# Order of the low parts, of the routing lists and of the blocks in a sliding-window attention and mixture-of-experts kernel

## The chip, the cores and the metric

The kernel runs on one core of one Trainium2 chip. The metric is the device time of one execution in microseconds; a run's time is compared by medians. One execution was also profiled.

## The reference

Attention over 8 batches, 8 heads, 576 positions and 64 dimensions with a window of 64 positions, then a mixture of 8 experts over the 4608 rows that come out, each row going to its two best experts:

```python
scores = scale * np.matmul(q, k.transpose(0, 1, 3, 2))
mask = (rel >= 0) & (rel < window)
attn = softmax(np.where(mask, scores, -1e9));  x = rows of attn @ v      # N=4608, DM=512
noisy_logits = x @ w_gate + np.log1p(np.exp(x @ w_noise)) * noise
top2, top2_w = the two largest of 8 and their softmax
for e in range(E):
    h = np.maximum(x[mask] @ w1[e], 0.0)                                 # 512 -> 1024
    out[mask] += top2_w[mask, k, None] * (h @ w2[e])                     # 1024 -> 512
```

## The kernel before

Attention and routing take the first 193 us and are not touched. What follows is 8 layers, one an expert, the experts 1 to 7 in the order of their load. A layer e has three chunks c of 384, 384 + tail and 384 rows (the tail has 64 rows in layers 0 to 2, 32 in layers 3 and 4, none in layers 5 to 7). A chunk (e,c) is an *up* (`up`, L799) and a *down* (`down`, L863).

Every product is made of three matmuls: high by high, high by low, low by high. A high part is ScalarE's copy of a value into fp32r (`split`, L214), the low part is VectorE's subtraction of the high one from the value (L215). So each value that goes into a matmul has an ACT instruction and, behind it, a DVE instruction that waits for it.

The up has 8 pieces `o` of 4 steps of 3 matmuls (L820 to L822), each piece into one of three `ps_u` banks. After a piece ACT writes `hh` (L826), DVE `hl` (L830, L832), and for the tail `ht` (L834, L835). In layers 1 to 7 the chunks 1 and 2 are *paired*: two row tiles are multiplied in seven blocks instead of eight halves. For these, `raw` (L841, L844 to L847) and its parts `sh`, `sl` (L848 by way of `split`) are made in the up, and `th`, `tl` from sums of the weights (`mix_w2`, L224).

The down is, unpaired, one `whole` (L876) for each row tile of 128 rows. Paired, it is first the tail's `whole`, then the blocks `p2` and `p`, then four steps of the third tile, the blocks of `s0`, `p5`, `s1` and `s3`, the rest of the third tile, and the last block. The three `ps_d` banks are handed out in the order in which `acc_bank` is called, and so are the three `yo` row tiles. The tail's result is read by ACT (L895) and then by DVE (L896); a block's result is scaled by ACT (`scaled`, L927) or scaled and added by DVE (`added_to`, L930). `add_rows` (L853) adds a row tile into the output by an indirect DMA on POOL.

A chunk's rows are gathered by indirect DMAs on POOL (`gather`, L733), five of them in the down two chunks earlier and the rest in the up of the chunk before, and turned in the down before the chunk's own up (`turn`, L751): a transpose `xy` by DVE (L760), `xh` by ACT (L772), `xl` by DVE (L775).

The list of rows of the expert of rank r is made by `top_list` (L621): 23 small DVE instructions, 9 marks (one-hot tiles, L664), 36 small matmuls over the marks (`put`, L658), then `no`, `hi`, `lo` (L676 to L678; the profile calls `hi` and `lo` `thi` and `tlo`), eight tiny matmuls (`four`, L684, L685) and the index tile `ixs` (L691). It is a generator in `pending`, advanced by `drain` (L978): each call takes n instructions from it; a number that it yields makes it pass over so many calls; `due` holds matmuls with the call at which they are issued. After attention a number is first looked up in `LATE`.

All order is written out by hand: `spread` (L75) sends the steps of an up or a down to PE and, between them, the side work of `parts` at the share of the steps that each part names. Each engine works through its own instructions in the order of the program. The loop over the chunks (L1216) puts the side work together: weight cuts, turns, gathers, mixes, weight loads on SP's queue and the drains.

Of the kernel before, what the change touches and what calls it, by code (L numbers as in the profile page):

```python
# [59 lines left out]
HALF = 8  # L60
# [25 lines left out]
def tile_kernel(ctx, tc, qT, kT, vx, wgx, noise, w1, w2, out):  # L86
# [133 lines left out]

    def split_w2():
        return [lambda f=f: split(stage[:, f % 4, f // 4], W2["h"][:, f], W2["l"][:, f]) for f in ORDER]

    def mix_w2(i):  # L224
        x = stage[:, i].rearrange("p a (b d) -> p a b d", b=2)
        sums = [(x[:, 0, 0], x[:, 0, 1], x[:, 0, 0]), (x[:, 0, 1], x[:, 1, 1], x[:, 0, 1]),
                (x[:, 1, 1], x[:, 1, 1], x[:, 0, 0]), (x[:, 1, 0], x[:, 1, 0], x[:, 1, 1])]
        return ([lambda t=t: nc.vector.tensor_tensor(*t, op=OP.subtract) for t in sums]
                + [lambda a=a: split(stage[:, i, a], W2["th"][:, i, a], W2["tl"][:, i, a]) for a in range(2)])
# [391 lines left out]
    def top_list(e):  # L621
# [38 lines left out]
        for a in range(0, NT, HALF):  # L660
            b = min(NT, a + HALF)
            t = exa.tile([128, 4, 128], F32, name="xy", bufs=2).bitcast(BF).rearrange("p a (b l) -> p (a b) l", l=128)
            for q in range(a, b, 4):
                yield lambda q=q, t=t, a=a: nc.vector.tensor_tensor(  # L664
                    t[:, q - a:q - a + 4], lane[:, None, :].to_broadcast([128, 4, 128]),
                    ln[:, q:q + 4, None].to_broadcast([128, 4, 128]), op=OP.is_equal)
            due.append((calls[0] + LATE["due"], lambda t=t, a=a, b=b: put(t, a, b)))
        yield LATE["due"] + 2
# [12 lines left out]
        def four():  # L681
            for g in range(4):
# [3 lines left out]
        due.append((calls[0] + 2, four))  # L686
# [3 lines left out]
        yield 3  # L690
        yield lambda: nc.vector.tensor_scalar(ALL["ix"][:, e - 1].rearrange("p z g -> p g z"), all4, 4.0, quarter,  # L691
                                              op0=OP.mult, op1=OP.add)

    pending, due, gath = [], [], []
    PACE = {}

# [54 lines left out]
    def turn(e, c):  # L751
# [17 lines left out]

        def g(q, m):  # L770
            h, l = (x[:, :, q * 128:q * 128 + m].rearrange("p k (t c) -> p k t c", c=32) for x in (xh, xl))
            nc.scalar.activation(h, cur[q], AF.Copy)  # L772
            if work.index((e, c)) > 3:
                PACE["t"] = xh.bitcast(F32)[0:1, 0, q * 128:q * 128 + 1]
            nc.vector.tensor_tensor(l, cur[q], h.bitcast(F32), op=OP.subtract)  # L775
        return [lambda q=q, m=m, x=x: x(q, m) for q, m in tiles(e, c) for x in (f, g)]
# [22 lines left out]
    def up(e, c):  # L799
# [6 lines left out]
        raw = {}  # L806
        for o in range(KF):
# [25 lines left out]
            if tail:  # L833
                nc.scalar.activation(t[:, 0], p[:, main:n], AF.Relu)  # L834
                nc.vector.scalar_tensor_tensor(t[:, 1], p[:, main:n], 0.0, t[:, 0].bitcast(F32),  # L835
                                               op0=OP.max, op1=OP.subtract)
            if mix:
                i = f % 4
                if f < 4:
                    x = raw[i] = MIX["p"].tile([128, 4, 128], F32, name="raw", bufs=2)  # L840
                    nc.scalar.activation(x[:, 0:2], p[:, 0:256].rearrange("p (r c) -> p r c", r=2), AF.Relu)  # L841
                else:
                    x = raw.pop(i)
                    nc.vector.scalar_tensor_tensor(x[:, 2], p[:, 128:256], 0.0, x[:, 1], op0=OP.max, op1=OP.add)  # L844
                    nc.vector.tensor_tensor(x[:, 1], x[:, 0], x[:, 1], op=OP.subtract)
                    nc.vector.tensor_tensor(x[:, 0], x[:, 2], x[:, 0], op=OP.subtract)
                    nc.vector.scalar_tensor_tensor(x[:, 3], p[:, 0:128], 0.0, x[:, 0], op0=OP.max, op1=OP.subtract)  # L847
                    split(x, *(y[:, i] for y in SH[e, c]))  # L848
            yield
# [13 lines left out]
    def down(e, c):  # L863
# [12 lines left out]
        def whole(q, m):  # L876
            wt, y, p = weight(q, m), row_tile(), acc_bank()
# [28 lines left out]
        for q, m in tiles(e, c)[3:]:  # L906
            yield from whole(q, m)
# [3 lines left out]
        ws, ys = [weight(q, 128) for q in range(2)], [row_tile() for _ in range(2)]  # L911
# [34 lines left out]
        scaled(lo, p, 0)  # L946
        added_to(lo, p2, 0)
        yield
        for _ in range(4):
            next(third)  # L950
            yield
# [3 lines left out]
        p5 = acc_bank()[:, lo]  # L955
# [22 lines left out]
    def drain(n, bank=True):  # L978
# [3 lines left out]
        while n and pending and calls[0] > calls[1]:  # L982
# [233 lines left out]
    for n, (e, c) in enumerate(work):  # L1216
# [17 lines left out]
        elif n == 1:  # L1234
            pending.extend([start(2), count(), top_list(1), count2()])
            side += [lambda: drain(3), lambda: (drain(3), drain_slots(1, gath))] * 16
        elif c == 0:
            side += split_w2()
        elif c == 1 and e:
            parts0.append((0.0, 0.6, mix_w2(3) + [lambda: load_w1(e + 1, slice(3, 4))]))  # L1240
# [13 lines left out]
        if last and e + 1 < E:  # L1254
            cuts = split_w1()
            for i in range(4):
                side += cuts[2 * i:2 * i + 2] + [lambda i=i: load_w2(e + 1, i)]
# [79 lines left out]
```

## Time and profile before

| | |
|---|---|
| median of 3 runs | 1084.17 us (1082.07 to 1087.49) |
| the profiled execution's own time | 1082.79 us |
| its span, first to last instruction | 1081.1 us |
| PE, matmuls | 1006.5 us busy, 93% |
| PEld, weight loads | 902.6 us, 83% |
| DVE | 707.1 us, 65% |
| ACT | 473.8 us, 44% |
| POOL | 537.0 us, 50% |

The engines are PE (TensorE's matmuls), PEld (its weight loads), DVE (VectorE), ACT (ScalarE), POOL (GpSimd) and SP (SyncE, here only a DMA queue). A tile's name stands before `<-`, what it is made from behind it; L and a number is a line of the kernel before. A matmul's end is modelled, so matmuls overlap in a timeline, and their starts are what counts. An engine that is not the bound may stand idle at no cost.

### The profile page before, as it was taken

The page shows a single profiled execution, that of the slowest core. Times are in us where ns is not written, and L with a number is a line of the kernel's source. Part 1 is how long each engine was busy: PE and PEld are TensorE (multiplying, and loading weights), DVE is VectorE, ACT ScalarE, POOL GpSimd, SP SyncE. Part 2 cuts the span into 40 slices and gives each one's busy share as a digit, 9 for nine tenths or more (in the row PEclk, how much of TensorE's full clock was granted, in tenths as well). Part 3 has the DMA queues.
Part 4 walks back from the last instruction along what each step waited for, and adds up shares of the span by engine and source line. Part 5 has one row for each costly group of instructions (what it writes and reads, how often), then busy time and mean ns, then how long its engine had stood idle before and what let it go on. Part 6 is the DMA issues. An engine that isn't in the chain of part 4 may idle for free.

```text
span 1081.1 us, 23842 instructions
## 1 busy us (share of the span) xinstructions
PE 1006.5 (93%) x9253; PEld 902.6 (83%) x9253; DVE 707.1 (65%) x1716; ACT 473.8 (44%) x1141; POOL 537.0 (50%) x763
## 2 busy tenths in 40 slices
PE   8888889989999899989998999989999999999996
PEld 7777778878898789878987889888898888989895
DVE  6668887773866766666666767576668666467541
ACT  4877784312344344432544245324443453354331
POOL 5432230313865457636663757455666465656411
PEclk9999999989999999999999999999999999999998
DMA  9877897632434134513541344314353335342222
GB/s 318 264 243 230 264 325 272 183 117 38 108 85 108 32 74 106 110 42 47 130 104 48 52 111 86 87 28 106 68 130 50 102 69 115 54 114 48 43 33 30
DMA packets 60667, 123.62 MB, mean 114 GB/s; under 512 B 9728, under 2 KB 9856, under 8 KB 60416
## 3 DMA queue, kind: packets, MB, share of 16 engines
q1 hardware_dynamic: 40816, 83.18, 23.5%
q0 software_dynamic: 19728, 38.82, 21.2%
q8 instruction: 75, 1.23, 0.5%
q14 instruction: 48, 0.39, 0.1%
HBM read 81.59 MB, written 40.37 MB: 113 GB/s over the span
## 4 chain that ended last, share of the span: by engine, by line
PE 56%; DVE 21%; ACT 9%; issue 9%; DMA 3%; POOL 2%; DVEq 0%; ACTq 0%; POOLq 0%
PE ps_d L881 7%; PE ps_d L882 7%; PE ps_d L883 7%; PE ps_u L821 7%; PE ps_u L820 6%; PE ps_u L822 6%; DMA xg<-xrows,ixs 3%; PE ps_d L937 3%; PE ps_d L936 2%; PE ps_d L935 2%; DVE sl L215 2%; DVE hl L832 2%; PE ps_o L334 2%; ACT sh L214 2%; ACT hh L826 2%
## 5 line engine op out<-in xcount | busy, mean ns | idle before, releaser
L746 POOL DMA_INDIRECT xg<-xrows,ixs x258 | 273.4, 1060 | 70.0 <-issue 59.8
L820 PE MATMUL ps_u<-xh,w1h 128*128 128x384 f32 (+2 forms) x752 | 261.6, 348 | 9.8 <-ACT xh L772 5.2
L821 PE MATMUL ps_u<-xl,w1h 128*128 128x384 f32 (+2 forms) x752 | 256.8, 342 | 1.7 <-DVE xl L775 1.7
L822 PE MATMUL ps_u<-xh,w1l 128*128 128x384 f32 (+2 forms) x752 | 256.3, 341 | 0.0
L855 POOL DMA_INDIRECT out_dram<-yo,lts x67 | 118.1, 1763 | 96.4 <-DVE yo L930 54.2
L820 PEld LDWEIGHTS ps_u<-xh,w1h 128*128 128x128 f32 x752 | 141.7, 188 | 17.3 <-ACT xh L772 6.5
L881 PE MATMUL ps_d<-w2h,hh 128*128 128x512 f32 x352 | 141.0, 401 | 12.2 <-DVE yo L896 12.2
L821 PEld LDWEIGHTS ps_u<-xl,w1h 128*128 128x128 f32 x752 | 141.8, 189 | 5.0 <-DVE xl L775 3.2
L832 DVE SCALAR_TENSOR_TENSOR hl<-ps_u,hh 128x384 fp32r<-128x384 f32 x132 | 73.5, 557 | 110.6 <-ACT hh L826 95.6
L826 ACT ACTIVATE hh<-ps_u 128x384 fp32r<-128x384 f32 x188 | 91.4, 486 | 122.4 <-PE ps_u L822 106.6
L822 PEld LDWEIGHTS ps_u<-xh,w1l 128*128 128x128 f32 x752 | 141.6, 188 | 1.5
L882 PE MATMUL ps_d<-w2l,hh 128*128 128x512 f32 x352 | 139.5, 396 | 0.3 <-issue 0.3
L883 PE MATMUL ps_d<-w2h,hl 128*128 128x512 f32 x352 | 139.2, 396 | 0.0
L881 PEld LDWEIGHTS ps_d<-w2h,hh 128*128 128x128 f32 x352 | 67.4, 191 | 25.5 <-DVE yo L896 13.0
L299 POOL TENSOR_TENSOR t<-t,mx 128x512 f32<-128x512 f32 x36 | 37.5, 1042 | 98.9 <-DVE mx L298 74.8
L745 POOL COPY spacer<-hh 1x1 f32<-1x1 f32 x155 | 40.3, 260 | 86.6 <-ACT hh L826 84.9
L883 PEld LDWEIGHTS ps_d<-w2h,hl 128*128 128x128 f32 x352 | 67.2, 191 | 14.4
L214 ACT ACTIVATE sh<-raw 128x512 fp32r<-128x512 f32 x56 | 35.4, 632 | 99.2 <-DVE raw L847 77.3
L882 PEld LDWEIGHTS ps_d<-w2l,hh 128*128 128x128 f32 x352 | 67.3, 191 | 13.2 <-issue 0.7
L772 ACT ACTIVATE xh<-xy 128x512 fp32r<-128x512 f32 (+2 forms) x67 | 41.1, 613 | 71.6 <-DVE xy L760 64.0
L215 DVE TENSOR_TENSOR sl<-raw,sh 128x512 fp32r<-128x512 f32 x56 | 38.8, 692 | 42.4 <-ACT sh L214 37.1
L745 POOL COPY spacer<-xh 1x1 f32<-1x1 f32 x55 | 20.2, 367 | 87.4 <-ACT xh L772 87.2
(273 smaller groups left out, 2056.9 us busy)
## 6 DMA issues: line engine op xcount, KB each, us to landing
stage<-in_w_dram SPq DMA_DIRECT2D x56, 512.0 KB
out_dram<-zero SPq DMA_DIRECT2D x40, 256.0 KB
vw<-in_vx_dram SPq DMA_DIRECT2D x36, 260.0 KB
qc<-in_qT_dram SPq DMA_DIRECT2D x36, 256.0 KB
KW<-in_kT_dram SPq DMA_DIRECT2D x36, 256.0 KB
xrows<-x SPq DMA_DIRECT2D x36, 256.0 KB
xg<-xrows,ixs POOLq DMA_INDIRECT x258
stage<-in_w_dram SPq DMA_DIRECT2D x8, 256.0 KB
```

Source lines behind the costliest of these rows:

```text
L215: eng.tensor_tensor(l, s, h.bitcast(F32), op=OP.subtract)
L745: nc.gpsimd.tensor_copy(spacer, PACE["t"])
L746: nc.gpsimd.indirect_dma_start(out=XG[e, c, t // 4][:, t % 4, :], out_offset=None, in_=XQ[:(DUMP + seen.get((e, c), NT) * 128) * 4], in_of ...
L820: nc.tensor.matmul(p[:, :n], lhsT=w1h[:, k, fs], rhs=xh[:, k, :n], start=(k == 0), stop=False)
L821: nc.tensor.matmul(p[:, :n], lhsT=w1h[:, k, fs], rhs=xl[:, k, :n], start=False, stop=False)
L822: nc.tensor.matmul(p[:, :n], lhsT=w1l[:, k, fs], rhs=xh[:, k, :n], start=False, stop=(k == KD - 1))
L826: nc.scalar.activation(h, p[:, :main], AF.Relu)
L832: nc.vector.scalar_tensor_tensor(l, p[:, :main], 0.0, h.bitcast(F32), op0=OP.max, op1=OP.subtract)
L855: s = nc.gpsimd.indirect_dma_start(out=out[:DUMP + seen.get((e, c), NT) * 128], out_offset=bass.IndirectOffsetOnAxis(ap=slot(e, c, q)[:m, ...
L881: nc.tensor.matmul(p, lhsT=hh[f][:, sl], rhs=w2h[:, f, :], start=(f == 0), stop=False)
L882: nc.tensor.matmul(p, lhsT=hh[f][:, sl], rhs=w2l[:, f, :], start=False, stop=False)
L883: nc.tensor.matmul(p, lhsT=hl[f][:, sl], rhs=w2h[:, f, :], start=False, stop=(f == KF - 1))
```

## The change

- `turn`: in layers 1 to 7 the low part `xl` becomes a step of its own, behind `xh`. Turns are spread over the first 0.75 of the down, not 0.9, and the weight cuts of the next layer beside them over 0.95, where the two followed each other.
- `staged`: weight cuts put out the high part of a piece and then the low part of the piece before. The loads that follow a piece are issued behind its low part.
- `up`: the tail's high part and, for f below 4, `raw` are issued on ACT ahead of DVE's `hl`; the low part of `sh` is owed until the next piece has its `hl`.
- `down`, paired: the third tile's first four steps lead, then the tail, then `p`, `p2` and the rest in the old order. `p2` and `p5` are the two halves of one bank. The row tiles of the two paired tiles are taken after the tail's and the third's.
- `top_list`: marks come in groups of four (`HALF`), one group in three calls, with their matmuls three calls (`PUT`) behind; `four` is due after four calls instead of two. The calls are drawn out from two stretches, down (e,1) and up (e,2), to four: down (e,1) 22 calls, up (e,2) 22, down (e,2) 14, up (e+1,0) 28. The first list is made in chunk (0,1) with two instructions a call.

```diff
-HALF = 8
+HALF = 4
+PUT = 3
+    def staged(cuts, after=lambda k: None):
+        def item(k):
+            if k < len(cuts):
+                nc.scalar.activation(cuts[k][1], cuts[k][0], AF.Copy)
+            if k:
+                nc.vector.tensor_tensor(cuts[k - 1][2], cuts[k - 1][0], cuts[k - 1][1].bitcast(F32), op=OP.subtract)
+                after(k - 1)
+        return [lambda k=k: item(k) for k in range(len(cuts) + 1)]
+    def cut_w1(e):
+        cuts = [tuple(x[:, k, c:c + 512] for x in (w1s, w1h, w1l)) for k in range(KD) for c in range(0, F, 512)]
+        return staged(cuts, lambda k: load_w2(e + 1, k // 2) if k % 2 else None)
...
         for a in range(0, NT, HALF):
...
+            t = exa.tile([128, HALF, 128], BF, name="hot", bufs=2)
+            yield lambda t=t, a=a: nc.vector.tensor_tensor(
+                t, lane[:, None, :].to_broadcast([128, HALF, 128]),
+                ln[:, a:a + HALF, None].to_broadcast([128, HALF, 128]), op=OP.is_equal)
+            due.append((calls[0] + PUT, lambda t=t, a=a: put(t, a, a + HALF)))
+            yield 1
+        yield PUT + 1
...
-        due.append((calls[0] + 2, four))
+        due.append((calls[0] + 4, four))
...
-        yield 3
...
+        yield 6
...
+        steps = (f, g, g2) if e else (f, both)
+        return [lambda q=q, m=m, x=x: x(q, m) for q, m in tiles(e, c) for x in steps]
...
             PACE["t"] = h.bitcast(F32)[0:1, 0:1]
+            if tail:
+                nc.scalar.activation(t[:, 0], p[:, main:n], AF.Relu)
             if mix and f < 4:
+                x = raw[f] = MIX["p"].tile([128, 4, 128], F32, name="raw", bufs=2)
+                nc.scalar.activation(x[:, 0:2], p[:, 0:256].rearrange("p (r c) -> p r c", r=2), AF.Relu)
...
-            if mix:
+            for y in owed:
+                nc.vector.tensor_tensor(*y, op=OP.subtract)
+            owed.clear()
+            if mix and f >= 4:
...
-                    split(x, *(y[:, i] for y in SH[e, c]))
+                nc.scalar.activation(sh, x, AF.Copy)
+                owed.append((sl, x, sh.bitcast(F32)))
...
-        for q, m in tiles(e, c)[3:]:
-            yield from whole(q, m)
+        ends = [whole(q, m) for q, m in tiles(e, c)[3:]]
         third = whole(2, 128)
...
-        ws, ys = [weight(q, 128) for q in range(2)], [row_tile() for _ in range(2)]
+        ws, ys = [weight(q, 128) for q in range(2)], []
...
-        p2 = acc_bank()[:, lo]
-        yield from block(p2, of_h(0, 1), of_w(1, lo))
-        yield
+        for _ in range(4):
+            next(third)
+            yield
+        for x in ends:
+            yield from x
+        ys += [row_tile() for _ in range(2)]
         p = acc_bank()[:, lo]
         yield from block(p, of_h(0, 0), of_w(0, lo))
         scaled(lo, p, 0)
+        yield
+        both = acc_bank()
+        p2, p5 = both[:, lo], both[:, hi]
+        yield from block(p2, of_h(0, 1), of_w(1, lo))
         added_to(lo, p2, 0)
         yield
-        for _ in range(4):
-            next(third)
-            yield
         yield from block(p, of_s(0), of_t(1, hi), False)
         scaled(hi, p, 0)
         yield
-        p5 = acc_bank()[:, lo]
...
-            side += [lambda: drain(3), lambda: (drain(3), drain_slots(1, gath))] * 16
+            side += [lambda: drain(2), lambda: (drain(2), drain_slots(1, gath))] * 16
         elif c == 0:
-            side += split_w2()
+            side += cut_w2()
...
+        if c == 0 and 0 < e < E - 1:
+            parts0.append((0.0, 1.0, [lambda: drain(1)] * 28 + [settle]))
...
-            parts0.append((0.0, 1.0, [lambda: drain(1)] * (30 if e == 0 else 28) + [settle] * (e > 0)))
+            parts0.append((0.0, 1.0, [lambda: drain(1)] * (22 if e else 32)))
...
-        parts = [(0.3, 0.95, side) if nxt and nxt[0] == 0 else (0.0, 0.9, side)]
+        parts = [(0.3, 0.95, side) if nxt and nxt[0] == 0 else (0.0, 0.75, side)] + parts0
...
-            parts.append((0.0, 1.0, [lambda: drain(4)] * 24 + [settle]))
+            parts.append((0.0, 1.0, [lambda: drain(2)] * 32 + [lambda: have(1)]))
...
-            parts.append((0.0, 1.0, [lambda: drain(1)] * 28))
-        if n == 2:
-            parts.append((0.0, 0.9, [lambda: drain(1)] * 24 + [settle]))
+            parts.append((0.0, 1.0, [lambda: drain(1)] * 22))
+        if last and e < E - 2:
+            parts.append((0.0, 1.0, [lambda: drain(1)] * 14))
```

## Rows read from the trace of the kernel before

**Rows 1.** The page: span, busy time and share of each engine.
```profile
span 1081.1 us, 23842 instructions
PE 1006.5 (93%) x9253; PEld 902.6 (83%) x9253; DVE 707.1 (65%) x1716; ACT 473.8 (44%) x1141; POOL 537.0 (50%) x763
```

**Rows 2.** PE's waits: who waited for whom, us in total, times, longest.
```profile
PE ps_d L881 <- DVE yo L896: 12.2, 4, 3.1
PE ps_g L684 <- DVE thi L677: 8.0, 5, 1.6
...
PE ps_u L820 <- ACT xh L772: 5.2, 6, 0.9
PE ps_d L935 <- ACT hh L826: 4.2, 5, 1.3
PE ps_g L658 <- DVE xy L664: 4.1, 4, 2.2
PE ps_d L891 <- DVE ht L835: 3.8, 4, 1.0
PE ps_u L820 <- DVE raw L847: 2.6, 4, 0.9
PE ps_u L821 <- DVE xl L775: 1.7, 6, 0.3
```

**Rows 3.** PE's timeline: start, us, [idle before <- releaser]; up (3,2) and down (7,2).
```profile
619.22 0.34 PE L822 MATMUL ps_u<-xh,w1l 128*128 128x384 f32 x1
621.16 0.17 PE L684 MATMUL ps_g<-thi,same 128*128 128x10 bf16 x1 [1.61 <-DVE thi L677]
...
1056.86 0.28 PE L936 MATMUL ps_d<-w2l,hh 128*128 128x256 f32 x1
1057.23 0.39 PE L937 MATMUL ps_d<-w2h,hl 128*128 128x256 f32 x1
```

**Rows 4.** Windows: stretch, us, busy (x) of PE, PEld, DVE, ACT, POOL; granted clock; DMA.
```profile
233.10:263.20 30.10, 26.02 (x145) 20.25 (x145) 15.17 (x44) 4.58 (x9) 4.87 (x6) 0.89 0.28 68
476.00:482.00 6.00, 4.66 (x17) 3.82 (x18) 5.79 (x21) 0.63 (x1) 4.80 (x7) 0.72 0.26 39
...
606.90:627.40 20.50, 18.86 (x143) 17.76 (x142) 12.97 (x37) 6.41 (x14) 14.85 (x20) 1.00 0.40 62
```

**Rows 5.** Timelines of ACT and DVE in down (3,1), around the tail's read.
```profile
590.03 0.71 DVE L760 STREAM_TRANSPOSE xy<-xg 128x512 f32<-128x512 f32 x1
590.83 0.63 ACT L772 ACTIVATE xh<-xy 128x512 fp32r<-128x512 f32 x1 [1.44 <-DVE isit L625]
591.49 0.59 ACT L895 ACTIVATE yo<-ps_d 32x512 f32<-32x512 f32 x1
...
593.44 0.68 DVE L896 TENSOR_TENSOR yo<-yo,ps_d 32x512 f32<-32x512 f32 x1
```

**Rows 6.** Timelines of DVE and ACT, durations and steps, list work and start of down (3,2).
```profile
605.07 2.49 DVE L664 TENSOR_TENSOR xy<-lane,tln 128x512 bf16<-128x512 bf16 x4
...
628.45 0.56 DVE L832 SCALAR_TENSOR_TENSOR hl<-ps_u,hh 128x384 fp32r<-128x384 f32 x1 [0.83 <-ACT hh L826]
...
629.89 0.29 DVE L847 SCALAR_TENSOR_TENSOR raw<-ps_u,raw 128x128 f32<-128x128 f32 x1
630.28 0.63 ACT L214 ACTIVATE sh<-raw 128x512 fp32r<-128x512 f32 x1 [1.86 <-DVE raw L846]
630.94 0.69 DVE L215 TENSOR_TENSOR sl<-raw,sh 128x512 fp32r<-128x512 f32 x1 [0.76 <-ACT sh L214]
631.55 1.29 DVE L215 TENSOR_TENSOR w1l<-stage,w1h 128x512 fp32r<-128x512 f32 x2
631.86 0.46 ACT L927 ACTIVATE yo<-ps_d,lts 128x256 f32<-128x256 f32 x1
632.21 2.18 ACT L214 ACTIVATE w1h<-stage 128x512 fp32r<-128x512 f32 x4
```

**Rows 7.** Waits of all engines: ACT for DVE on one PSUM bank.
```profile
ACT ht L834 <- DVE hl L832: 26.1, 22, 5.5
```

More of the change, by code (lines that the diff above doesn't have):

```diff
@@ L227, in mix_w2 @@
                 (x[:, 1, 1], x[:, 1, 1], x[:, 0, 0]), (x[:, 1, 0], x[:, 1, 0], x[:, 1, 1])]
+        cuts = [(stage[:, i, a], W2["th"][:, i, a], W2["tl"][:, i, a]) for a in range(2)]
         return ([lambda t=t: nc.vector.tensor_tensor(*t, op=OP.subtract) for t in sums]
-                + [lambda a=a: split(stage[:, i, a], W2["th"][:, i, a], W2["tl"][:, i, a]) for a in range(2)])
+                + staged(cuts, lambda k: load_w1(e + 1, slice(i, i + 1)) if k else None))
     XQT = {}
@@ L660, in top_list @@
         for a in range(0, NT, HALF):
[L661 to L668, printed above, removed]
+            t = exa.tile([128, HALF, 128], BF, name="hot", bufs=2)
[5 more added lines that the diff above has]
+        yield PUT + 1
         if not ALL:
@@ L689, in top_list, with last @@
         yield lambda: nc.vector.tensor_tensor(w, w, a[:, 4], op=OP.add)
-        yield 3
-        yield lambda: nc.vector.tensor_scalar(ALL["ix"][:, e - 1].rearrange("p z g -> p g z"), all4, 4.0, quarter,
-                                              op0=OP.mult, op1=OP.add)
+        yield 6
+        def last():
+            nc.vector.tensor_scalar(ALL["ix"][:, e - 1].rearrange("p z g -> p g z"), all4, 4.0, quarter,
+                                    op0=OP.mult, op1=OP.add)
+            made.add(e)
+        yield last
     pending, due, gath = [], [], []
     PACE = {}
+    made = set()
     LT, XG, XH, XL, HH, SH, MIX = {}, {}, {}, {}, {}, {}, {}
@@ L774, in g, with g2, both @@
                 PACE["t"] = xh.bitcast(F32)[0:1, 0, q * 128:q * 128 + 1]
+        def g2(q, m):
+            h, l = halves(q, m)
             nc.vector.tensor_tensor(l, cur[q], h.bitcast(F32), op=OP.subtract)
-        return [lambda q=q, m=m, x=x: x(q, m) for q, m in tiles(e, c) for x in (f, g)]
+        def both(q, m):
+            g(q, m)
+            g2(q, m)
+        steps = (f, g, g2) if e else (f, both)
+        return [lambda q=q, m=m, x=x: x(q, m) for q, m in tiles(e, c) for x in steps]
     turns = [0]
@@ L805, in up @@
         mix = paired(e, c)
-        raw = {}
+        raw, owed = {}, []
         for o in range(KF):
@@ L876, in whole, with run @@
         def whole(q, m):
-            wt, y, p = weight(q, m), row_tile(), acc_bank()
+            return run(q, m, acc_bank(), row_tile())
+        def run(q, m, p, y):
+            wt = weight(q, m)
             if m == 128:
@@ L993, in drain, with have @@
                 pending.pop(0)
+    def have(e):
+        while e not in made:
+            drain(1)
     def settle():
@@ L1254, in tile_kernel @@
         if last and e + 1 < E:
-            cuts = split_w1()
-            for i in range(4):
-                side += cuts[2 * i:2 * i + 2] + [lambda i=i: load_w2(e + 1, i)]
+            parts0 = [(0.0, 0.95, cut_w1(e))]
+        else:
+            parts0 = []
         if nxt and n != 2:
             side += turn(*nxt)
-        parts = [(0.3, 0.95, side) if nxt and nxt[0] == 0 else (0.0, 0.9, side)]
+        parts = [(0.3, 0.95, side) if nxt and nxt[0] == 0 else (0.0, 0.75, side)] + parts0
         if n == 0:
@@ L1272, in tile_kernel @@
             pending.append(top_list(e + 2))
[L1273 to L1275 removed]
+            parts.append((0.0, 1.0, [lambda: drain(1)] * 22))
+        if last and e < E - 2:
+            parts.append((0.0, 1.0, [lambda: drain(1)] * 14))
         if c == 0 and e:
[L1277 removed]
+            parts.append((0.0, 1.0, [x for i in range(3) for x in mix_w2(e, i)]))
         if 1 < n < len(work) - 2:
```

35 lines of the change are left out of this document (19 added, 16 removed).

## The prediction

> **What bounds the kernel now.** I read the page first, then who TensorE waits for, then the timelines around those waits. On the page PE is busy 93% of a span of 1081.1 us [rows 1]; no other engine comes near, so time is won only where a matmul starts late. The view of PE's waits names the places [rows 2]. Eight rows carry the argument: together 41.8 us in 38 waits, all but list 1's in the layers after the first. They are: the third tile waiting for the tail's PSUM bank (12.2, four times); the four small matmuls of a list waiting for `thi` (8.0, five times); the next layer's first matmul waiting for `xh` and its second for `xl` (5.2 and 1.7, six times each); the first block of a down waiting for the last `hh` (4.2, five); list 1's marks (4.1, four); the tail waiting for its last `ht` (3.8, four); a PSUM bank of the next `f` held by `raw` (2.6, four).
>
> A wait costs more than its row: the gap is counted from the modelled end of the matmul before it. Around the list's four matmuls the starts lie 621.16 - 619.22 = 1.94 us apart where the step is 0.17, so 1.77 is lost where the row has 1.61 [rows 3]. I add 0.17 a wait: 41.8 + 38 x 0.17 = 48.3 us. Waits under 0.15 us aren't listed; one that repeats is the first `hl` of a down, 1057.23 - 1056.86 = 0.37 for a step of 0.12 [rows 3]; there are nine such places: 2.2 us.
>
> Last, the clock. The granted clock was 0.89 over 30.1 us after list 1's waits and 0.72 over 6 us after one wait of the third tile [rows 4]; two more stretches look like the latter, one after another third tile, one after a `thi` wait. In such a stretch neighbouring matmuls are on the lower level, 1.2 GHz, after PE stood still. Lost at most 30.1 x 0.11 + 3 x 6 x 0.28 = 8.3 us.
>
> **The change part by part.** No matmul is added or removed, so the sum is over waits.
>
> *Order of a paired down.* The third tile's first four steps now lead (4 x 3 matmuls x 0.227 us = 2.7 us), then the tail, then the blocks. The first four steps use f = 0, 4, 1, 5, made long before, so the waits for the last `hh` (4.2 + 5 x 0.17 = 5.1), `hl` (2.2) and `ht` (4.5) have 2.7 us or more of cover and go.
>
> The third tile's 12.9 us go too, but a wait follows it. The third holds a bank, `p` the second, and `both` is the fourth bank asked for after tail, third and `p`: with three buffers, the tail's. Now the tail's read ends late because ACT was held by a copy of `xh` that waited for a transpose, and DVE by list work (L895 at 591.49, L896 at 593.44, the up having ended at 583.2) [rows 5]. In the new order, from the up's end: the last high part at 0.2, `ht` 0.6, `hl` 0.84, four `raw` of 0.3 to 2.7, ACT's `sh` 2.8, `sl` 3.4 to 4.0 (steps as in [rows 6]); then on DVE a transpose (4.7), four list items (6.2), the low part of `x` (6.8), two list items, the second transpose (8.1). ACT copies the second `xh` at 8.2 and only then the tail (8.7); L896 runs from 9.3 to 10.0. PE wants the bank at 2.7 + 3.7 + 1.4 = 7.9. New wait 2.2 us, in four downs: 8.8 us. Ends: 0 (DVE and ACT ahead) and 3.2 each, today's.
>
> *Blocks on one bank.* `s0` writes `p` again after ACT has scaled it, now behind one block of 1.4 us (12 x 0.12) instead of block and half a third tile; `p5` lies in the other half of `p2`'s bank. Whether a write there must wait for DVE's read of `p2`, in other columns, no row of before shows. If only columns count, the cost is 0. The nearest rows are those where ACT waits for DVE on one `ps_u` bank though both only read, and other columns: `ht` for `hl`, 26.1 us [rows 7]. So I take it that the bank orders them. The Trainium skill says so of PSUM (page "PSUM — Partial Sum Buffer", section "PSUM bank collisions raise a hardware error"): a dependency is put between any two instructions of different engines that touch one bank and quadrant, whatever the columns. By that rule `p5` waits, as my sum has it; by columns alone the time would come out some 7 us lower; no run here shows it yet.
>
> Price in the downs (e,2), layers 1 to 5, which have turns, cuts and list work. ACT after `sh` (2.6): a cut, `xh` (4.6, behind the transpose), two cuts at 0.54 each, then the scaling at 6.1, done at 6.6. PE reaches `s0` at 2.7 + 1.4 + 1.4, with two groups of marks 5.9: wait 0.7 to 0.8. DVE after `sl` (3.2): two transposes, two marks, three low parts of weights, one of `x`, eight pieces at 0.60 to 0.62 [rows 6], so the read of `p2` runs 8.7 to 9.2; PE wants `p5` at 8.1: 1.1. Together 1.9 x 5 = 9.5. Layer 6 (no list) 1.3. Down (5,1) has list work but no tail: 1.5. Downs (6,1), (7,1), (7,2) have neither: 0. Sum 12.3 us. Ends: 0, and 3.1 us a down, the longest wait of PE in the layers [rows 2].
>
> *Low parts behind high parts.* In the turn the low part becomes a step of its own, and the turn ends at 0.75 of the down (15 of 22 steps), beside the weight cuts instead of behind them; today it starts after twelve items. The waits for `xh` and `xl` (6.9 + 12 x 0.17 = 8.9) go, with 4 us to spare. SP's queue: `load_w2` now follows each second cut, up to step 19; its last piece is needed eleven us later. POOL's gathers keep their place; the last of a chunk lands before the third transpose (step 11, some 8 us in). In the up, `ht` and `raw` move ahead of `hl` on ACT, which ends the waits of [rows 7], and `sl` goes behind the next `hl`: DVE no longer stands 0.76 us for ACT's `sh`. `raw`'s hold on the bank (2.6 + 0.7 = 3.3) goes: last read at 2.5 us, needed at 4.2.
>
> *Lists.* `four` comes four drains behind and two calls later starts on light DVE work: 8.0 + 0.9 = 8.9 us go. Marks become nine groups of four, three calls apart, read by PE four calls later (some 3 us in an up). Seven marks in each up (e,2) fit DVE: its 12.97 us there [rows 4] lose the small items and gain about three marks of 0.62 [rows 6], some 14.5 against 17. Finer groups cost some 0.15 us a list: 1.0. For list 1, marks start in the first up and DVE is 2 to 3 us behind: one wait of 1.2 stays of 4.1 + 0.7 = 4.8.
>
> *Sum.* 48.3 + 2.2 + clock 5 (of 8.3, since waits of over 2 us remain in four downs) - 8.8 - 12.3 - 1.2 - 1.0 = 32.2 us. The profiled execution took 1082.8 us, its span and 1.7 around it; 1082.8 - 32.2 = 1050.6. It lies 1.4 below the median of the runs, so I predict 1052.
>
> **The rivals.** *Waits hidden:* ACT and DVE run ahead, since nothing stalls them any more; the 8.8 + 12.3 go: 1031. For it: DVE is busy 65% on the whole. Against: the order at each down's start is a chain, not a load. *Dear waits:* DVE comes 1 to 2 us later to the start of each down than I count: 10 downs x 1.2 + 4 x 0.5 more, 1066. *DVE as the bound:* seven marks leave DVE no slack in the five ups (e,2), PE waits for `ps_u` banks, up to 4 us each: 1072; with dear waits as well 1086, no change. That is also the time if the low parts change places without ending a wait. *Slower:* one mechanism, the read of `p2` on DVE in each of the 14 paired downs. It decides above (32.2 + 5.4) / 14 = 2.7 us more than I count, over 4 us a down; then over 1090. Against it: no wait of PE in the layers is that long today, and three of the downs have nothing queued there.
>
> **How the numbers follow.** Forecast 1052: 0.58. Waits hidden, 1031: 0.17. Dear waits, 1066: 0.11. DVE bound, 1072: 0.04; with dear waits, no change: 0.06. Slower: 0.04. Faster by over 0.5% (about what a measurement here can tell from no change) 0.90, within 0.06, slower 0.04. The range leaves out part of the hidden case and all beyond dear waits: 1033 to 1068.
>
> **What would show it.** Right: no wait of L881 for L896 and of L684 for `thi`; up (e+1,0) starting without a gap; a new PE wait for L896 of about 2 us in four downs, and in (e,2) waits of a block for ACT's scaling and for DVE's read, about 1 us each. No `p5` wait at all would mean that columns order the bank. Wrong: waits of L820 for `raw` in (e,2), or of L658 for marks. The sum is wrong if those new waits exceed 3 us, or if the clock falls as often as before.

## The result, and the profile after

The changed kernel takes 1056.16 us (median of 4 runs, 1052.7 to 1060.8) against 1085.83 of the kernel before (4 runs beside it): a ratio of 0.9734, 95% interval 0.9684 to 0.9783, or 29 us less. The forecast was 1052, range 1033 to 1068. The total came out, and so did the new waits. What the prediction said of where the old waits come from did not, as the runs below show.

The profiled execution took 1060.8 us, the longest of the four. Its page:

```profile
span 1059.1 us, 23858 instructions
PE 1002.3 (95%) x9253; PEld 903.4 (85%) x9253; DVE 694.5 (66%) x1716; ACT 465.6 (44%) x1141; POOL 539.4 (51%) x763
```

PE's matmuls are the same 9253; the engines' sums hardly differ from [rows 1]. Of the 22 us of span, 4.2 went out of PE's busy time and the rest out of its idle time. The view of PE's waits (us in total, times, longest):

```profile
PE ps_d L977 <- DVE yo L939: 9.5, 4, 2.8
...
PE ps_d L977 <- ACT yo L969: 5.8, 9, 0.9
PE ps_d L977 <- DVE yo L972: 4.5, 6, 0.8
PE ps_g L676 <- DVE hot L680: 2.2, 2, 1.5
PE ps_u L852 <- PEq L1255: 2.2, 1, 2.2
...
PE ps_d L924 <- ACT hh L858: 0.5, 1, 0.5
```

(L852 to L854 are the up's matmuls, L924 to L926 those of a `whole`, L977 to L979 those of a block; L939 is DVE's read of the tail, L969 ACT's scaling, L972 DVE's scaled addition, L680 the marks, L858 `hh`. A run's lines are those of its own kernel, so they differ a little from run to run.) Of the eight rows of [rows 2] only marks are left, 1.5 us of list 1's; 0.7 us more for marks and the 0.5 us for an `hh` are new, both in down (0,2). In their place stand the three `ps_d` rows that the prediction foresaw, 19.8 us in 19 waits.

The first down begins at 193.86 us in the profile before and at 197.37 in this one. Attention and routing are not touched by the change; their length differs from execution to execution (190.9 to 197.4 over the profiles of this case). From the first down to the end of the span it is 887.2 us before and 861.7 after: 25.5 us of change in the code that changed. The table below gives this time for each run too, since it is free of that scatter; it is one profiled execution each.

### The profile page after: what moved, and what is told of

The parts are those of the page before. It is cut to its first block, busy times and chain, and to the rows that moved or that the text cites. A ratio compares the mean times of both kernels' runs of the same rounds, so it can differ in the third digit from the quotient of the medians.

```text
span 1059.1 us, 23858 instructions
## 1 busy us (share of the span) xinstructions
PE 1002.3 (95%) x9253; PEld 903.4 (85%) x9253; DVE 694.5 (66%) x1716; ACT 465.6 (44%) x1141; POOL 539.4 (51%) x763
## 4 chain that ended last, share of the span: by engine, by line
PE 63%; DVE 16%; issue 8%; ACT 6%; DMA 3%; POOL 1%; another core or an unknown queue 1%; DVEq 0%; ACTq 0%; POOLq 0%
PE ps_u L852 9%; PE ps_u L854 8%; PE ps_u L853 8%; PE ps_d L924 6%; PE ps_d L926 6%; PE ps_d L925 6%; PE ps_d L977 3%; DMA xg<-xrows,ixs 3%; PE ps_d L978 3%; PE ps_d L979 3%; PE ps_o L352 3%; PE ps_s L293 2%; ACT sh L883 2%; ACT hh L858 2%; DVE hl L868 1%
## 5 line engine op out<-in xcount | busy, mean ns | idle before, releaser
L767 POOL DMA_INDIRECT xg<-xrows,ixs x258 | 281.3, 1090 | 72.1 <-issue 61.5
L852 PE MATMUL ps_u<-xh,w1h 128*128 128x384 f32 (+2 forms) x752 | 260.8, 347 | 2.2 <-PEq L1255 2.2
L854 PE MATMUL ps_u<-xh,w1l 128*128 128x384 f32 (+2 forms) x752 | 256.4, 341 | 0.0
L858 ACT ACTIVATE hh<-ps_u 128x384 fp32r<-128x384 f32 x188 | 91.7, 488 | 161.5 <-PE ps_u L854 132.5
L895 POOL DMA_INDIRECT out_dram<-yo,lts x67 | 109.8, 1639 | 87.0 <-DVE yo L972 38.5
L852 PEld LDWEIGHTS ps_u<-xh,w1h 128*128 128x128 f32 x752 | 141.7, 188 | 4.2 <-issue 2.4
L854 PEld LDWEIGHTS ps_u<-xh,w1l 128*128 128x128 f32 x752 | 141.7, 188 | 1.4
L924 PE MATMUL ps_d<-w2h,hh 128*128 128x512 f32 x352 | 139.2, 395 | 0.5 <-ACT hh L858 0.5
L926 PE MATMUL ps_d<-w2h,hl 128*128 128x512 f32 x352 | 137.9, 392 | 0.0
L866 DVE SCALAR_TENSOR_TENSOR hl<-ps_u,hh 128x256 fp32r<-128x256 f32 x56 | 23.8, 424 | 110.5 <-ACT raw L864 107.3
L926 PEld LDWEIGHTS ps_d<-w2h,hl 128*128 128x128 f32 x352 | 66.1, 188 | 14.2 <-DVE hl L868 0.3
L924 PEld LDWEIGHTS ps_d<-w2h,hh 128*128 128x128 f32 x352 | 66.2, 188 | 12.9 <-ACT hh L858 1.0
L925 PEld LDWEIGHTS ps_d<-w2l,hh 128*128 128x128 f32 x352 | 66.1, 188 | 12.8 <-issue 0.8
L766 POOL COPY spacer<-hh 1x1 f32<-1x1 f32 x137 | 36.1, 264 | 73.1 <-ACT hh L858 53.4
L929 ACT ACTIVATE yo<-ps_d,lts 128x512 f32<-128x512 f32 x35 | 24.1, 689 | 96.7 <-PE ps_d L926 51.0
L766 POOL COPY spacer<-xh 1x1 f32<-1x1 f32 x66 | 23.5, 356 | 83.8 <-ACT xh L796 82.7
```

What stands on the lines that cost most here:

```text
L766: nc.gpsimd.tensor_copy(spacer, PACE["t"])
L767: nc.gpsimd.indirect_dma_start(out=XG[e, c, t // 4][:, t % 4, :], out_offset=None, in_=XQ[:(DUMP + seen.get((e, c), NT) * 128) * 4], in_of ...
L852: nc.tensor.matmul(p[:, :n], lhsT=w1h[:, k, fs], rhs=xh[:, k, :n], start=(k == 0), stop=False)
L854: nc.tensor.matmul(p[:, :n], lhsT=w1l[:, k, fs], rhs=xh[:, k, :n], start=False, stop=(k == KD - 1))
L858: nc.scalar.activation(h, p[:, :main], AF.Relu)
L895: s = nc.gpsimd.indirect_dma_start(out=out[:DUMP + seen.get((e, c), NT) * 128], out_offset=bass.IndirectOffsetOnAxis(ap=slot(e, c, q)[:m, ...
```

## The experiments

Medians in us; the ratio is to runs of the kernel before on the same chip (1084.11, 1083.53 and 1085.25 in the three groups; 13, 13 and 7 runs).

| run | what it is | median (runs) | ratio, 95% | first down to end |
|---|---|---|---|---|
| before | | 1085.83 (4) | 1 | 887.2 |
| after | | 1056.16 (4) | 0.9734 (0.9684-0.9783) | 861.7 |
| old_lows | after, old low-part order in up, turns, cuts and mixes | 1091.05 (10) | 1.0064 (1.0041-1.0087) | 898.0 |
| old_up | after, old `up` alone | 1086.51 (10) | 1.0022 (1.0006-1.0038) | 891.8 |
| lows_only | before, new low-part order alone | 1047.61 (4) | 0.9664 (0.9618-0.9709) | 853.9 |
| owed_only | after, high parts behind `hl` again | 1065.12 (4) | 0.9832 (0.9792-0.9872) | 872.0 |
| act_first | after, `sl` no longer owed | 1053.71 (4) | 0.9705 (0.9672-0.9739) | 857.7 |
| old_turn | after, old turns and cuts | 1054.03 (4) | 0.9725 (0.9694-0.9756) | 859.2 |
| old_lists | after, old lists | 1052.05 (4) | 0.9687 (0.9636-0.9739) | 859.0 |
| old_down | after, old order of a paired down | 1044.35 (4) | 0.9624 (0.9574-0.9673) | 849.8 |
| third_early | after, rest of the third tile before `p2` | 1030.89 (4) | 0.9500 (0.9448-0.9553) | 836.3 |
| early_old_lists | third_early, old lists | 1034.53 (4) | 0.9544 (0.9514-0.9575) | 839.1 |
| p5_same_columns | after, `p5` in the columns of `p2` | 1051.14 (1) | - | 854.6 |

My theory at first was the prediction's own: each part ends the waits that it was costed with, the new order of the down most of them. The rival: the waits are ends of one delay that arises elsewhere, and one part carries the gain.

**old_lows.** All low parts back in their old places, lists and down as changed (the same lines as in old_up below, and in `turn` and the cuts):

```diff
-        steps = (f, g, g2) if e else (f, both)
+        steps = (f, both)
...
-                nc.scalar.activation(sh, x, AF.Copy)
-                owed.append((sl, x, sh.bitcast(F32)))
+                    split(x, *(y[:, i] for y in SH[e, c]))
```

> The changed kernel with low parts right behind their high parts again (splits, mixes, cuts and turns as before, turns behind the cuts to 0.9 of the down, up's ACT and DVE order as before), all else as changed. Theory A: waits for xh and xl (8.9 us) and for raw (3.3) come back, and since DVE comes 2.5 us later to each down, the waits for the tail's bank, s0 and p5 grow by 1 to 2.5 us each: 1075 to 1090. Rival (each term stands by itself): 1068, with bank waits as in after.

Measured: 1091.05, a little slower than the kernel before (0.6%) and just above both theories' times. With lists and down changed and the low parts not, nothing is won: without the low parts' order there is no gain.

**old_up.** Only the up's order is put back: `hl` ahead of `ht` and `raw` on ACT, `sl` right behind `sh`.

```diff
-            if tail:
-                nc.scalar.activation(t[:, 0], p[:, main:n], AF.Relu)
-                x = raw[f] = MIX["p"].tile([128, 4, 128], F32, name="raw", bufs=2)
...
-                nc.scalar.activation(sh, x, AF.Copy)
-                owed.append((sl, x, sh.bitcast(F32)))
+                    split(x, *(y[:, i] for y in SH[e, c]))
```

> The changed kernel with the up's order of before alone (ht and raw behind hl on ACT, sl right behind sh); turns, cuts, mixes, lists and down as changed. Theory A (the up's order carries what old_lows gave back, since DVE comes late to everything behind an up): waits for raw (2.5 us) and for marks (up to 13) are back and bank waits are some 5 us larger, xh and xl stay gone: 1070 to 1082. Rival (turns and cuts carry it): within 5 us of after, 1052 to 1061.

Measured: 1086.51, dearer than either theory had it. The gain is gone with the `up` alone; by the medians the turns, cuts and mixes of old_lows add 4.5 us to it. Its waits of PE (L931 is the read of the tail, L961 the scaling, L964 the scaled addition):

```profile
PE ps_d L969 <- DVE yo L931: 18.6, 4, 4.7
PE ps_g L676 <- DVE hot L680: 12.5, 7, 2.9
PE ps_d L969 <- ACT yo L961: 7.9, 7, 1.7
...
PE ps_d L969 <- DVE yo L964: 3.8, 5, 0.8
PE ps_u L852 <- ACT raw L873: 2.0, 4, 0.7
```

None of the up's own banks is more than 2 us of it; the price of the up's order is paid in the down behind it (the tail's bank, 4.7 us at most) and by the marks. These five rows come to 44.8 us where the changed kernel has 22.0 in the same places, 22.8 of the 30.1 us between the two kernels' stretches. The waits for `thi`, `xh`, `xl`, `ht` and a block's `hh` are not back, though the up is the old one: the new lists, turns and down do end them by name, and the delay comes out in other waits. So it sits on DVE and ACT. Their timelines show it. Before, up (7,2), which has neither tail nor side work (start, us, [idle before <- releaser]; each engine from its own view, put in order of start):

```profile
1047.91 0.56 DVE L832 SCALAR_TENSOR_TENSOR hl<-ps_u,hh 128x384 fp32r<-128x384 f32 x1 [0.83 <-ACT hh L826]
...
1049.36 0.29 DVE L847 SCALAR_TENSOR_TENSOR raw<-ps_u,raw 128x128 f32<-128x128 f32 x1
1049.74 0.63 ACT L214 ACTIVATE sh<-raw 128x512 fp32r<-128x512 f32 x1 [1.86 <-DVE raw L847]
1050.40 0.69 DVE L215 TENSOR_TENSOR sl<-raw,sh 128x512 fp32r<-128x512 f32 x1 [0.76 <-ACT sh L214]
1051.01 0.42 DVE L830 SCALAR_TENSOR_TENSOR hl<-ps_u,hh 128x256 fp32r<-128x256 f32 x1
1051.46 0.39 ACT L841 ACTIVATE raw<-ps_u 128x256 f32<-128x256 f32 x1 [0.71 <-DVE hl L830]
1051.74 0.49 ACT L826 ACTIVATE hh<-ps_u 128x384 fp32r<-128x384 f32 x1
1052.26 0.56 DVE L832 SCALAR_TENSOR_TENSOR hl<-ps_u,hh 128x384 fp32r<-128x384 f32 x1 [0.83 <-ACT hh L826]
```

Read it as a closed ring: `hl`, four sums `raw` on DVE, `sh` on ACT, `sl` on DVE, the next piece's `hl` on DVE, only then ACT's `raw` on the same bank, ACT's `hh` of the piece after, and `hl` again. Each starts when the one before is done, and PE is nowhere in it: 1052.26 - 1047.91 = 4.35 us for two pieces, where PE takes 4.16. So in a paired up DVE and ACT fall back by 0.19 us a pair, and every other instruction that they are given there comes on top. The same two pieces after, in up (7,2):

```profile
1026.38 0.56 DVE L868 SCALAR_TENSOR_TENSOR hl<-ps_u,hh 128x384 fp32r<-128x384 f32 x1
...
1028.21 0.63 ACT L883 ACTIVATE sh<-raw 128x512 fp32r<-128x512 f32 x1 [1.86 <-DVE raw L882]
1029.11 0.37 ACT L864 ACTIVATE raw<-ps_u 128x256 f32<-128x256 f32 x1
1029.52 0.42 DVE L866 SCALAR_TENSOR_TENSOR hl<-ps_u,hh 128x256 fp32r<-128x256 f32 x1 [1.41 <-ACT raw L864]
1029.86 0.68 DVE L873 TENSOR_TENSOR sl<-raw,sh 128x512 fp32r<-128x512 f32 x1
1030.01 0.49 ACT L858 ACTIVATE hh<-ps_u 128x384 fp32r<-128x384 f32 x1 [0.52 <-PE ps_u L854]
1030.54 0.56 DVE L868 SCALAR_TENSOR_TENSOR hl<-ps_u,hh 128x384 fp32r<-128x384 f32 x1
```

The step is 4.16, PE's own, and `hh` waits 0.52 us for PE: the ring is open, and ACT stands ready at the up's end. With a tail the ring is longer. In old_up's up (3,1), on DVE's timeline:

```profile
578.19 0.56 DVE L864 SCALAR_TENSOR_TENSOR hl<-ps_u,hh 128x384 fp32r<-128x384 f32 x1 [0.73 <-ACT hh L858]
...
581.74 0.68 DVE L227 TENSOR_TENSOR tl<-stage,th 128x512 fp32r<-128x512 f32 x1
...
584.04 0.56 DVE L864 SCALAR_TENSOR_TENSOR hl<-ps_u,hh 128x384 fp32r<-128x384 f32 x1 [0.83 <-ACT hh L858]
...
589.31 0.56 DVE L864 SCALAR_TENSOR_TENSOR hl<-ps_u,hh 128x384 fp32r<-128x384 f32 x1 [0.83 <-ACT hh L858]
```

One pair takes 589.31 - 584.04 = 5.27 us, and 5.85 with a single `tl` put between; the whole up (3,1) takes 17.92 us in the changed kernel, 4.48 a pair. That is 0.8 to 1.4 us lost a pair.

**lows_only.** The kernel before with the new low-part order, nothing else: the lists and the down are before's (in the diff, what it takes from before):

```diff
-HALF = 4
+HALF = 8
...
+        p2 = acc_bank()[:, lo]
+        yield from block(p2, of_h(0, 1), of_w(1, lo))
...
         for _ in range(4):
             next(third)
             yield
-        for x in ends:
-            yield from x
```

> The kernel before with the new order of the low parts alone (up, turns, cuts, mixes); its own down and its own lists. Theory A (this part alone carries the whole gain and more): third tile's waits of 1 to 2 us four times, none for hh, ht, xh, raw or thi: 1038 to 1047. Rival (each part has its own gain): half of the gain or less, 1062 to 1072.

Measured: 1047.61, ratio 0.9664, just outside the first theory's range and far from the rival's. The low parts' order alone brings at least as much as all parts together (the two intervals overlap a little; from the first down to the end it is 853.9 us, after 861.7). With the lists and the down of before, the waits for `thi`, `xh`, `xl`, `ht`, `raw` and a block's `hh` are gone all the same. Not all goes: the third tile still waits for the tail's bank, 7.7 us in four waits where it had 12.2, and list 1's marks are waited for 2.6 us where it was 4.1. The new `up` by itself, without turns, cuts and mixes, was not put into the kernel before.

**owed_only.** The high parts `ht` and `raw` go back behind `hl` on ACT; `sl` stays owed.

```diff
-            if tail:
-                nc.scalar.activation(t[:, 0], p[:, main:n], AF.Relu)
...
                 nc.vector.scalar_tensor_tensor(l, p[:, :main], 0.0, h.bitcast(F32), op0=OP.max, op1=OP.subtract)
             if tail:
+                nc.scalar.activation(t[:, 0], p[:, main:n], AF.Relu)
...
+            if mix and f < 4:
+                x = raw[f] = MIX["p"].tile([128, 4, 128], F32, name="raw", bufs=2)
```

> The changed kernel with ACT's order of before in the up (ht and raw behind hl); sl stays owed to the next piece, all else as changed. Theory A (ring): hl, raw sums, sh, hh behind it on ACT, hl, raw, hh, hl, some 4.15 us, just PE's own 4.16, so that every mark, mix or tail is paid in lag: 1062 to 1082, between after and old_up. Rival (the 0.76 us in which DVE stood for sh was the trouble): as after, 1050 to 1060.

**act_first.** The other half: `sl` follows `sh` at once, the high parts stay ahead.

```diff
-                nc.scalar.activation(sh, x, AF.Copy)
-                owed.append((sl, x, sh.bitcast(F32)))
+                split(x, sh, sl)
```

> The changed kernel with sl again right behind sh in the up; ht and raw stay ahead of hl on ACT, all else as changed. Theory A (ring: in an up of before each pair of pieces is a closed ring between ACT and DVE of 4.35 us where PE needs 4.16, read from hl to hl in up (7,2) of before; with raw ahead of hl the ring is hl, raw sums, sh, sl, hl, some 3.5 us, under PE's): DVE keeps up, 1050 to 1062, as after. Rival (the owed sl is what frees DVE): ring over 4.16, 1070 to 1087.

Measured: owed_only 1065.12, act_first 1053.71, the changed kernel 1056.16. Without the first half some 9 us are lost, without the second nothing: issuing ACT's reads of a bank ahead of DVE's read is enough to open the ring. In owed_only's up (7,2), on DVE's timeline, DVE waits for `hh` in every pair; the step is 4.13, PE's, but with little left over:

```profile
1030.15 0.56 DVE L864 SCALAR_TENSOR_TENSOR hl<-ps_u,hh 128x384 fp32r<-128x384 f32 x1 [0.24 <-ACT hh L858]
...
1034.28 0.56 DVE L864 SCALAR_TENSOR_TENSOR hl<-ps_u,hh 128x384 fp32r<-128x384 f32 x1 [0.24 <-ACT hh L858]
```

and with side work it falls behind: PE waits for the tail's bank 17.4 us in four waits, against 9.5. The first half alone (act_first) brings the whole gain, the second alone (owed_only) some 18 of the 29 us; the two don't add up.

**old_turn.** `xl` right behind `xh`, turns behind the cuts and up to 0.9 of the down.

```diff
-        steps = (f, g, g2) if e else (f, both)
+        steps = (f, both)
...
-            parts0 = [(0.0, 0.95, cut_w1(e))]
...
-        parts = [(0.3, 0.95, side) if nxt and nxt[0] == 0 else (0.0, 0.75, side)] + parts0
+        parts = [(0.3, 0.95, side) if nxt and nxt[0] == 0 else (0.0, 0.9, side)]
```

> The changed kernel with turns and weight cuts of before alone (xl right behind xh, low cuts right behind high cuts, turns behind the cuts up to 0.9 of the down); the up, mixes, lists and down as changed. Theory A: waits for xh and xl come back (8.9 us), the waits of s0 in the downs (e,2) fall, since four cuts but no transpose lie ahead of the scaling on ACT: 1060 to 1066. Rival (order of the up alone is enough, since xh and xl were late because the up's end was late): within 3 us of after.

Measured: 1054.03, the same as after. Its waits of PE:

```profile
PE ps_d L977 <- DVE yo L972: 5.4, 6, 0.9
PE ps_u L852 <- ACT xh L796: 4.9, 6, 0.9
PE ps_d L977 <- DVE yo L939: 4.9, 3, 1.9
...
PE ps_d L977 <- ACT yo L969: 2.5, 3, 0.8
PE ps_u L853 <- DVE xl L802: 1.7, 6, 0.3
...
PE ps_d L977 <- DVE tln L652: 1.1, 1, 1.1
```

The `xh` and `xl` waits are back as priced (6.6 us against 6.9 before), so the turn does end them, as the prediction had it. But the four `ps_d` rows come to 13.9 us where the three of the changed kernel have 19.8: the turns that were moved to the front of the down stand ahead of the reads that free the banks. What was won at the down's end was given back at its start, and the 4 to 10 us that the first theory allowed for were not there.

**old_lists.** Marks, `four` and drains as before.

```diff
-HALF = 4
+HALF = 8
...
-        due.append((calls[0] + 4, four))
+        due.append((calls[0] + 2, four))
```

> The changed kernel with lists made as before (marks in groups of eight in tiles shared with the turns, due six calls later; four two calls later; two stretches), all else as changed. Theory A (each term stands by itself): the waits for thi (8.9 us) and most of list 1's (3) come back: 1066 to 1069. Rival (the low parts' order alone makes DVE early enough): waits for thi under 0.5 us each, within 3 us of after.

Measured: 1052.05; from the first down to the end 859.0 us against 861.7. The theory that priced the lists at some 10 us falls. There is no wait for `thi` in its trace, nor in that of lows_only, whose lists are before's too: once the up's ring was open, DVE was no longer late for the list.

**old_down.** The paired down in its old order: tail, `p2`, `p`, four steps of the third, and banks for each.

```diff
+        p2 = acc_bank()[:, lo]
+        yield from block(p2, of_h(0, 1), of_w(1, lo))
...
         for _ in range(4):
             next(third)
             yield
-        for x in ends:
-            yield from x
-        ys += [row_tile() for _ in range(2)]
...
+        p5 = acc_bank()[:, lo]
```

> The changed kernel with the down of before (tail, p2, p, third tile's first half; p5 in a bank of its own turn), all else as changed. Theory A (the low parts' new order is what ends the waits for hh, hl and ht; the new down order only swaps the third tile's wait for waits on banks): sl of the up ends near 4 us after the up instead of 6.9, so hh, hl and ht are in time without cover, the third tile waits 1 to 2 us four times (6.5 us), and the waits of s0 (5.8 us in the trace of after) and p5 (4.5) go: faster than after by 8 to 15 us, some 1045. Theory B (the third tile's lead is what covers them): the 12.9 + 5.1 + 2.2 + 4.5 us of before come back and 20 us of new waits go: about 1061, and waits of L881's line for the tail's read of 3 us in the trace.

Measured: 1044.35, 12 us better than after, as the first theory had it. Its waits of PE on the down (L936 is the read of the tail, L967 the scaling):

```profile
PE ps_d L921 <- DVE yo L936: 6.2, 4, 2.0
PE ps_d L975 <- ACT yo L967: 4.7, 8, 0.8
PE ps_d L977 <- DVE hl L868: 1.9, 3, 0.6
```

12.8 us against 19.8. The waits for `hh` and `ht`, which the third tile's lead was to cover, do not come back without it. They too were DVE's and ACT's lateness out of the up. Only the late `hl` does, 1.9 us in three places.

**third_early.** The rest of the third tile (2.7 us of matmuls) moves from the down's end to just ahead of `p2`, so that the bank, the scaling and the sum have 2.7 us more.

```diff
         scaled(lo, p, 0)
         yield
+        yield from third
         both = acc_bank()
...
-        yield from third
         yield from block(p, of_h(1, 1), of_t(1, lo), False)
```

> The changed kernel with the rest of the third tile (2.7 us of matmuls) moved ahead of p2's block, so that the tail's bank, the scaling of p and the read of p2 have 2.7 us more before PE needs them. Theory A (the 19 waits on banks, 9.5 + 5.8 + 4.5 us in the trace of after, are chains of a fixed length from the up's end): they shrink to under 0.5 us each, the last block waits up to 0.5 us for the read of p: 1036 to 1044. Rival (DVE and ACT are behind throughout the down): the waits move to s1, s3 and the last block, within 5 us of after.

Measured: 1030.89, ratio 0.9500 (0.9448 to 0.9553), the best of all and 5 us below the first theory's range. PE's waits from the layers:

```profile
PE ps_u L852 <- PEq L1255: 2.6, 1, 2.6
PE ps_g L676 <- DVE hot L680: 2.2, 2, 1.5
...
PE ps_d L977 <- DVE yo L972: 0.5, 1, 0.5
```

Of the 19 bank waits one is left. The 25.4 us between the two kernels' stretches (861.7 and 836.3) are 19.3 us of these rows, 18 x 0.17 = 3.1 by the modelled ends, and 3.0 us that are not told apart. The clock has a share in these: from the first down to the end PE is busy 821.0 us instead of 827.0 for the same 4869 matmuls.

**early_old_lists.** third_early with the old lists (the edit of old_lists):

> third_early with lists made as before. Theory A (the low parts' order alone ends the waits for thi; the drawn-out lists only move 1 to 3 us about): within 4 us of third_early, 1028 to 1035, no wait for thi over 0.5 us. Rival (the lists' order is worth its 8.9 us once the bank waits no longer hide it): 1038 to 1042.

Measured: 1034.53, within the first theory's range. The intervals of the two ratios (0.9544 and 0.9500) overlap, so a worth of the new lists isn't shown here either; if there is one, it is about 4 us, on a kernel whose other waits are gone.

**p5_same_columns.** Does the bank or do the columns hold `p5`?

```diff
-        p2, p5 = both[:, lo], both[:, hi]
+        p2, p5 = both[:, lo], both[:, lo]
```

> The changed kernel with p5 in the very columns of p2 instead of the other half of its bank. Theory A (the bank orders PE's write behind DVE's read, whatever the columns): the six waits of p5 for DVE's read of p2 stay as they are, 0.7 to 0.9 us each, 4.5 us in all, the time as after within its spread. Rival (after's waits come from elsewhere in DVE's queue, columns decide): more or longer waits here, 14 of them, 1 us or more each.

Measured, in a single run: the waits of the paired downs are the same to the last digit as in the changed kernel:

```profile
PE ps_d L977 <- DVE yo L939: 9.5, 4, 2.8
...
PE ps_d L977 <- ACT yo L969: 5.8, 9, 0.9
PE ps_d L977 <- DVE yo L972: 4.5, 6, 0.8
```

So in these kernels PE's write to one half of a bank waits for DVE's read of the other half just as it does for a read of its own half. Whether the chip asks for it or only the dependencies in the program, which may go by the whole bank, these two runs don't tell. With the same waits this run is also the changed kernel's twin for the question of the clock below.

## Why the prediction was right, and where it was not

*The sum.* By the trace of after, term by term: waits ended 50.5, since of the waits so counted only list 1's marks are left, which stand below; clock 1 to 2, not 5 (see below); tail's bank 10.2, not 8.8 (starts of matmuls: 2.15 us lost in downs (1,1) and (2,1), 2.94 in (3,1) and (4,1)); `s0` and `p5` 12.7, not 12.3; list 1 1.7, not 1.2, two waits in down (0,2) that were not foreseen, for an `hh` and for marks, 1.6; the wait behind PE's own queue 0.7 longer. What the finer groups of marks cost, 1.0 in the prediction, was not measured. Without the clock that is 50.5 - 10.2 - 12.7 - 1.7 - 1.6 - 0.7 = 23.6, and with it some 25, of the 25.5 us from the first down to the end. All terms but the clock's were about right.

*The new waits in a paired down: right, by the chain.* In down (3,2), which begins at 614.2, the prediction had ACT's scaling at 6.1 us and DVE's read at 8.7. The timelines of ACT, DVE and PE:

```profile
620.47 0.45 ACT L969 ACTIVATE yo<-ps_d,lts 128x256 f32<-128x256 f32 x1
620.98 0.38 PE L977 MATMUL ps_d<-th,sh 128*128 128x256 f32 x1 [0.48 <-ACT yo L969]
622.89 0.47 DVE L972 SCALAR_TENSOR_TENSOR yo<-ps_d,lts,yo 128x256 f32<-128x256 f32 x1
623.42 0.38 PE L977 MATMUL ps_d<-th,sh 128*128 128x256 f32 x1 [0.75 <-DVE yo L972]
```

6.3 and 8.7. The waits came to 0.64 and 0.92 in each down (e,2) of layers 1 to 5, where 0.7 to 0.8 and 1.1 were given. Wrong was the nothing for downs without list work: (6,1) and (7,1) lose 0.98 at `s0`, as (5,1) does; in (7,1) the scaling stands on ACT behind `sh` and a copy of `xh` that waits 1.44 us for its transpose, and the transpose on DVE behind `sl`, with no list in it. That the bank orders `p5` was taken from [rows 7] and holds. The rule of the Trainium skill named beside it (page "PSUM — Partial Sum Buffer", section "PSUM bank collisions raise a hardware error") agrees with these runs: 4.5 us in six waits, with other columns and with the same.

*Where the old waits come from: wrong.* This is the step that failed. The prediction took each row of [rows 2] as its own fault and gave the third's, `hh`'s, `hl`'s and `ht`'s 24.7 us to the order of the down, `xh`'s and `xl`'s 8.9 to the turn, `thi`'s 8.9 to the lists, and to the up only `raw`'s 3.3 us. Only the turn's share held: with the old turn `xh` and `xl` are waited for again (old_turn). The up's order put back alone takes the whole gain away, 30 us where its term was 3.3 (1086.51). The low parts' order made alone, with the down and the lists of before, ends the waits for `thi`, `hh` and `ht` as well and a third of the third tile's (1047.61). The ring of 4.35 us against PE's 4.16 stood in the trace of before. Its sign in the waits of all engines is ACT's wait for `hl` before it may read the same bank for `raw` (us in total, times, longest):

```profile
ACT raw L841 <- DVE hl L830: 36.8, 35, 2.7
```

I had read its neighbour, [rows 7], and of the 26.1 us there 16.5 lie in eight waits of up (0,1), which is not paired. I took it for the rule on banks and wrote that the order "ends the waits", without asking what ACT's and DVE's lateness at the up's end costs in the down behind it. Most of the rows had one source: five rows whole or in part (`thi`, `hh`, `ht`, `raw`, the third's) end with the low parts' order alone.

*The parts that were priced as gains.* The new order of the down costs about 12 us (1056.16 against 1044.35) where the prediction had 24.7 gained and 21.1 paid. Turns and cuts are worth nothing that can be told (1054.03), since they move the bank waits by as much as they end; the lists are not either (1052.05). That the total still came out has one cause: the waits that were counted as ended did end, whichever part ended them, and the waits that were counted as new were counted from the chain itself. All parts were in the change, so the total could not show that the gain was given to the wrong ones; in that it was luck.

*The clock: mis-sized, and not the same in each execution.* The prediction gave back 5 us. In the profiled execution of after four stretches from the first down on held time at the lower clock. The view by windows (us; busy of PE, PEld, DVE, ACT, POOL; granted clock; DMA share, GB/s):

```profile
462.50:485.40 22.90, 20.92 (x126) 19.11 (x125) 16.50 (x45) 5.72 (x11) 11.13 (x15) 0.93 0.15 26
572.70:596.20 23.50, 20.72 (x126) 18.02 (x125) 16.68 (x45) 6.20 (x14) 11.55 (x16) 0.93 0.13 22
683.50:707.20 23.70, 20.93 (x126) 18.23 (x125) 16.69 (x45) 6.18 (x14) 11.19 (x16) 0.93 0.13 22
1015.70:1034.00 18.30, 18.30 (x97) 18.29 (x98) 7.61 (x21) 6.09 (x14) 0.95 (x2) 0.91 0.20 30
```

The first three are downs (2,1), (3,1) and (4,1), each with PE's wait for the tail's bank of 2.15 to 2.94 us in it, and the last is the up behind the wait for PE's queue. By the granted clock these stretches lost at most 22.9 x 0.07 + 23.5 x 0.07 + 23.7 x 0.07 + 18.3 x 0.09 = 6.6 us, those of before at most 8.3: 1 to 2 us given back. In p5_same_columns, with the same waits of the down, from the first down to the last matmuls the clock falls in one down alone, (4,1), with 0.91 over 20 us, and PE is busy 821.8 us instead of 827.0: 5.2 us for the same matmuls. So the term is real and its size is a matter of the execution; what makes the clock fall behind one such wait and not behind the same wait of another execution is open.

*The rivals.* "Waits hidden" would have had no bank waits: 19.8 us of them are there. "DVE as the bound" put seven marks against PE in the ups (e,2): no PE wait for a `ps_u` bank is left. "Dear waits" needed 14 us more in the new waits than the forecast had; they came to 22.9 against 21.1. "Slower" needed over 4 us a down at the read of `p2`; PE loses at most 0.92 us there.

## What to carry to other kernels

Where two engines read one buffer in turns, follow the order of their instructions round until it closes and compare its length with the bound engine's period: a ring that is 5% longer shows up as waits in other places, each of which looks like a fault of its own. Before pricing waits one by one, ask of each late producer what made it late, and back to an engine that waits for none; when several parts of a change each seem to end some, undo them one at a time. Behind a phase whose last results go through a fixed chain of three engines, put as much independent matmul work as the chain is long before a bank is asked for again: moving 2.7 us of it in each of the 14 paired downs was worth 25 us here.

## What the runs showed of the hardware

In these kernels ACT and DVE that both only read one PSUM bank go one behind the other in the order of the program: before, ACT waited for DVE's `hl` 36.8 us with `raw` (L841) and 26.1 us with `ht`, whose columns are others [rows 7], and putting ACT's reads first was enough for the whole gain (1053.71). A write by PE waits for a read by DVE in the other half of the bank (up to 0.8 us, six times). The granted clock was 0.93 over downs with a wait of 2.15 to 2.94 us in three of four cases in one execution, and below 1.00 in one of four in another with the same waits.
